# The folded gate and value weights of the last two batch pairs: two engines write their halves where the batches read them, in place of a staging tile and four transfers

## The chip, the cores and the metric

The kernel runs on one core of a Trainium2 chip. The metric is the device time of one execution in microseconds. The core has TensorE (PE in the profile, with its weight loads as PEld), VectorE (DVE), ScalarE (ACT), GpSimd (POOL) and SyncE (SP), and 16 DMA engines that move data between the chip's main memory (DRAM here) and the on-chip buffer. TensorE writes its products into PSUM, from which ScalarE and VectorE read them.

## The reference

Three stages follow each other. The first is an attention with a small packed set of 32 rows per head; the second a gated layer with an RMS norm; the third a two-layer block.

```python
p_packed = sm_attn(p, k, v)                    # q, k, v: (8, 8, 576, 64), p: (8, 8, 32, 64)
x = sm_attn(q, p_packed, p_packed)             # then laid out as (4608, 512)
xn = x / sqrt(mean(x * x) + 1e-6) * rms_g
g, val = xn @ w_gate, xn @ w_val               # 512 -> 1536 each
x = (g * sigmoid(g) * val) @ w_out             # 1536 -> 512
h = x @ w_in                                   # 512 -> 2048
out = maximum(0.01 * h, h) @ w_out2            # 2048 -> 512
```

## The kernel before

**Exact products from two parts.** All large products are made from a high part and a low part of each operand: the helper `mm3` (line 106) issues high x high, low x high and high x low into one PSUM tile, so each product costs three matmuls (their line in the profile is L112). A split is one ScalarE copy to the rounded format (`act_copy`, line 128, L129 in the profile) and one subtraction (`sub`, line 136, L137) on VectorE or GpSimd.

**Folded weights.** The attention's output is the product of the attention rows with `p_packed`, and the kernel does not form it. It multiplies `p_packed` into `w_gate` and `w_val` first. For each pair of batches it keeps a factor tile `lpw` (high and low), and for each block `n` of 256 gate columns and 256 value columns it makes four pieces, `pw_piece` (line 832): one piece is a product of 128 x 128 factors with a 128 x 512 weight tile `w`, three matmuls into a PSUM tile `pwps`. Partitions 0 to 63 of a piece belong to one batch of the pair and partitions 64 to 127 to the other. What is read later is `pw[n, bb]`, one tile for each batch `bb`, with two buffers each.

**How a piece got there.** ScalarE writes the high part of `pwps` over the weight tile `w`, VectorE writes the low part beside it, and two DMAs issued by GpSimd (L858) copy each half's 64 partitions from `w` to the tile of its batch, 256 KB each. So `w` is busy until these DMAs have landed, and there are four buffers of `w`, into which SP loads the next pieces' weights (L763, 512 KB each, four pieces ahead).

**The stages around it.** There are four pairs of batches and six blocks `n` in each, so 24 blocks and 96 pieces. A block is worked off in four steps (two batches, two column halves). In each step `gv` (line 864) makes the gate product `g` and the value product `v` from `pw` and the attention rows `ath`/`atl`, 24 matmuls; ScalarE makes the sigmoid product of `g`, VectorE multiplies it with `v` into `sg`, ScalarE and GpSimd split that into `hh` and `hl`; `y_out` (line 887) then makes 24 matmuls `y<-hh,wo` and `y<-hl,wo` of the step before, and VectorE or ScalarE adds them to `y_acc` (L903, or L129 in a pair's first block). The pieces of block n+1 are made during block n: one after the first step, one after the second, two after the third, none after the fourth. `pwps` and `y` share four PSUM buffers.

The third pair begins after the stretch in which the first half of the last block's layer is worked off (names `zh`, `zo`, `zr`, `zgf`, `zgh`, `zgl`, `zob`), together with the attention of the last four batches; the first four pieces of the third pair and the splits of `ath` for its batches lie in the last steps of that stretch. In the profiled execution the third and fourth pair take from 953.5 to 1301 us. Then the other half of the last layer follows (names `h`, `o`).

**What sets the order.** The code names an order of steps, but the tile framework's scheduler lists the instructions of each engine from it by its own estimates; an engine then works through its list strictly in order, waiting at each instruction for what that needs. So an instruction that waits holds up all that stands behind it on its engine, SP's transfers included.

The weight tile is released and the destination is fixed by these lines:

```python
act_copy(st[:, 0, :], ps)                      # st is w: high part
sub(nc.vector, st[:, 1, :], ps, st[:, 0, :])   # low part
nc.gpsimd.dma_start(out=pw[n, bb][hs, u].bitcast(F32), in_=st[hs].bitcast(F32))
```

Of the kernel before, what the change touches and what calls it, by code (L numbers as in the profile page):

```python
# [26 lines left out]
LATER = (0, 22)  # L27
ZEND = 51
FAST = 8
FASTQ = 6  # L30
OWN = 1
HOLD = 2
# [7 lines left out]
def pack_attention_moe_kernel(  # L40
# [14 lines left out]
    nc = tc.nc  # L55
# [50 lines left out]
    def mm3(ps, terms, start=True, stop=True):  # L106
        seq = [t for hi, lo in (("h", "h"), ("l", "h"), ("h", "l")) for t in [(hi, lo)]]
        n = len(terms) * 3
        i = 0
        for a, b in seq:  # L110
            for (lh, ll), (rh, rl) in terms:
                mm = nc.tensor.matmul(  # L112
                    ps,
                    lhsT=lh if a == "h" else ll,
                    rhs=rh if b == "h" else rl,
                    start=start and i == 0,
                    stop=stop and i == n - 1,
                )
                i += 1
        return mm  # L120
# [7 lines left out]
    def act_copy(o, i, scale=1.0):  # L128
        nc.scalar.activation(out=o, in_=i, func=AF.Copy, scale=scale)  # L129
# [6 lines left out]
    def sub(eng, o, a, hi):  # L136
        eng.tensor_tensor(out=o, in0=a, in1=hi.bitcast(F32), op=ALU.subtract)  # L137
# [67 lines left out]
    def bank(name):  # L205
        return psA.tile([P, 1, 512], F32, tag="y", bufs=ybufs, name=name)
# [18 lines left out]
    def soft1(i):  # L225
# [4 lines left out]
        def keys():  # L230
# [5 lines left out]
            )  # L236
            if i >= FAST:
                st["kh"] = att.tile([P, NS, 2, T], F32R, tag="raw", bufs=raws, name="kh" + nm)
# [9 lines left out]
        def packs():  # L248
# [6 lines left out]
            nc.vector.transpose(out=st["pT"], in_=pm.rearrange("p h (j d) -> p j h d", j=2))  # L255
            if i >= FAST:
                st["ph"] = att.tile([P, 2 * P], F32R, tag="pm", bufs=1, name="ph" + nm)
# [3 lines left out]
        def scores():  # L261
# [4 lines left out]
            for n, (s1, cs) in enumerate(parts):  # L266
                for k_, c in enumerate(cs):
                    if i >= FAST:
                        ss = slice(c * CS, (c + 1) * CS)
# [84 lines left out]
        def packed_turn():  # L354
            PT = att.tile([P, 2, 4, NPK], F32, tag="PT", bufs=2, name="PT" + nm)
            nc.vector.transpose(out=PT, in_=st["Pm"].rearrange("p h (j d) -> p j h d", j=2))
            raw["P", b, u] = (st["Pm"], PT)
            if i >= FAST:
                Ph = att.tile([P, 2 * P], F32R, tag="Ph", bufs=2, name="Ph" + nm)
# [32 lines left out]
    def soft2(i):  # L392
# [14 lines left out]
        def queries(cs):  # L407
# [6 lines left out]
            if cs[-1] == 1:  # L414
                raw.pop(("q", b, u))
                if i >= FAST:
                    st["qh"] = att.tile([P, NS, 2, T], F32R, tag="raw", bufs=raws, name="qh" + nm)
# [5 lines left out]
        def scores(cs):  # L423
            Pm, PT = raw["P", b, u]
            sn = tile_of("sn", "sn", [P, NS, NPK])
            for s2, cs in banks("s2" + nm, b):
                for k_, c in enumerate(cs):
                    if i >= FAST:
                        ss = slice(c * CS, (c + 1) * CS)
# [56 lines left out]
        def turn(cs):  # L486
# [4 lines left out]
            )  # L491
            if i >= FASTQ:
                Pm = raw["P", b, u][0].rearrange("p h d -> p (h d)")
# [10 lines left out]
        def squares(cs, x):  # L504
# [18 lines left out]
            for xp, cs in banks(f"xp{x}" + nm, b):  # L523
                for k_, c in enumerate(cs):
                    if i >= FASTQ:
                        ds, ts = slice(x * P, x * P + P), slice(c * CH, c * CH + CH)
# [125 lines left out]
    def flush_store():  # L652
        if stores:
            o, t = stores.pop()
            nc.sync.dma_start(out=o, in_=t.bitcast(F32))
# [67 lines left out]
    def until(done):  # L723
        while not done():
            assert drip
            drain(1)
# [103 lines left out]
    pw = {}  # L830

    def pw_piece(i):
        if i >= NPAIR * NFG * KT:
            return
        until(lambda: ("s", i) in wq)
        n, kt = i // KT, i % KT
        pr = n // NFG
        u, x = kt // 2, kt % 2
        if kt == 0:
            for bb in range(2):  # L840
                pw[n, bb] = mlpa.tile(
                    [P, 2, 2, 2 * G * P], F32R, tag=f"pw{bb}", bufs=2, name=f"pw{n}{bb}"
                )
        w = wq.pop(("s", i))
        wh, wl = w[:, 0, :], w[:, 1, :]
        lh, ll = lpw[pr]
        ps = bank(f"pwps{i}")[:, 0, :]
        mm3(ps, [((lh[:, kt, :], ll[:, kt, :]), (wh, wl))])

        if stores and stores[0][1] is w:  # L850
            flush_store()
        st = w
        act_copy(st[:, 0, :], ps)
        sub(nc.vector, st[:, 1, :], ps, st[:, 0, :])
        for half in range(2):
            bb = half if x == 0 else 1 - half
            hs = slice(64 * half, 64 * half + 64)
            nc.gpsimd.dma_start(out=pw[n, bb][hs, u].bitcast(F32), in_=st[hs].bitcast(F32))  # L858
# [73 lines left out]
    for f_ in weights[:HOLD]:  # L932
# [6 lines left out]
        (split_wo, 0),  # L939
        (split_wo, 1),  # L940
        (pw_piece, 0),
        (pw_piece, 1),
        (split_w, 4),
        (pw_piece, 2),
        (split_w, 5),
        (pw_piece, 3),
# [170 lines left out]
    for si, (n, bb, c) in enumerate(steps):  # L1117
        pr, fg = n // NFG, n % NFG
# [269 lines left out]
```

## Time and profile before

| what | us |
|---|---|
| median of 3 runs | 1758.36 |
| lowest and highest of them | 1751.75, 1763.99 |
| the profiled execution | 1764.21 |
| its span, first to last instruction | 1762.3 |
| PE busy in it | 1668.8 (95%) |
| DVE, ACT, POOL busy | 915.4, 649.5, 474.4 |

Busy time is the time in which an engine executes instructions, the span's share in brackets. An engine that is busy for 95% over the whole can still stand idle in a stage; a row of the timeline gives behind an instruction, in square brackets, how long its engine had been idle before it and which instruction or transfer ended that.

### The profile page before, as it was taken

How to read it: one execution, taken by the hardware profiler on the slowest of the kernel's cores; microseconds unless marked ns; L12 is line 12 of the kernel's file. 1: busy time of each engine (PE TensorE's matmuls, PEld its weight loads, DVE VectorE, ACT ScalarE, POOL GpSimd, SP SyncE). 2: the span in 40 equal slices, each digit the busy share in tenths (PEclk: the TensorE clock that was granted, in tenths of full speed). 3: DMA queues.
4: the chain of work that ended last, by engine and by line, in shares of the span. 5: the costliest groups of instructions: out<-in, count | busy, mean ns of one | idle time of the engine just before them, and what ended most of it. 6: DMA issues, size and time to landing. Idle time of an engine off the chain costs nothing.

```text
span 1762.3 us, 24309 instructions
## 1 busy us (share of the span) xinstructions
PE 1668.8 (95%) x9252; PEld 1474.4 (84%) x9252; DVE 915.4 (52%) x1560; ACT 649.5 (37%) x1142; POOL 474.4 (27%) x462
## 2 busy tenths in 40 slices
PE   6788889998999999999999899989999999999997
PEld 5578789998998788888888899989998888888885
DVE  6866887776547787666643244324533323232221
ACT  3454654453325555444333322332322222222221
POOL 2454565654421232121223233433310000000000
PEclk9889999999999999999999999999999999999999
DMA  9874776799947463642318657776645101010000
GB/s 280 243 228 145 228 218 192 239 331 324 336 131 271 161 207 127 220 162 76 99 63 281 192 172 204 247 222 186 188 152 212 38 11 38 11 37 13 13 11 24
DMA packets 95527, 287.85 MB, mean 163 GB/s; under 512 B 13876, under 2 KB 20276, under 8 KB 91316
## 3 DMA queue, kind: packets, MB, share of 16 engines
q1 hardware_dynamic: 80052, 235.96, 40.1%
q0 software_dynamic: 15360, 50.34, 11.5%
q8 instruction: 73, 1.20, 0.3%
q14 instruction: 42, 0.34, 0.1%
HBM read 174.85 MB, written 61.08 MB: 134 GB/s over the span
## 4 chain that ended last, share of the span: by engine, by line
PE 75%; DMA 11%; DVE 7%; issue 3%; ACT 2%; POOL 1%; SPq 1%; DVEq 0%; ACTq 0%; POOLq 0%
PE h L112 13%; PE o L112 13%; PE y L112 11%; PE zh L112 8%; PE zo L112 8%; PE g L112 7%; PE v L112 6%; DMA pw<-w 3%; PE pp L335 2%; PE pwps L112 2%; DMA w_dram<-w 1%; PE s L112 1%; DMA v<-in_v_dram 1%; DMA w<-in_moe_w_val_dram 1%; DVE cvw L685 1%
## 5 line engine op out<-in xcount | busy, mean ns | idle before, releaser
L112 PE MATMUL y<-hh,wo 128*128 128x288 f32 x1536 | 271.9, 299 | 9.5 <-DVE w L137 5.0
L112 PEld LDWEIGHTS y<-hh,wo 128*128 128x128 f32 x1536 | 228.6, 190 | 15.9 <-DVE w L137 6.4
L112 PE MATMUL o<-w,gh 128*128 128x512 f32 x640 | 212.4, 392 | 0.0
L137 POOL TENSOR_TENSOR hl<-sg,hh 128x576 fp32r<-128x576 f32 x96 | 139.1, 1449 | 258.0 <-ACT hh L129 252.0
L903 DVE TENSOR_TENSOR y_acc<-y_acc,y 128x288 f32<-128x288 f32 x320 | 140.8, 449 | 124.6 <-PE y L112 123.8
L1300 DVE TENSOR_TENSOR gf<-r,h 128x512 f32<-128x512 f32 x80 | 54.9, 687 | 247.9 <-ACT r L129 247.9
L112 PE MATMUL zo<-w,zgh 128*128 128x512 f32 x512 | 173.0, 394 | 0.0
L112 PE MATMUL g<-ath,pw 128*128 128x288 f32 x768 | 145.6, 305 | 21.4 <-DMA pw<-w 17.8
L112 PE MATMUL h<-yh,w 128*128 128x512 f32 x640 | 162.5, 393 | 0.5 <-DVE y_acc L903 0.5
L112 PE MATMUL zh<-zyh,w 128*128 128x512 f32 x512 | 161.3, 393 | 1.6 <-DVE y_acc L903 1.6
L112 PE MATMUL y<-hl,wo 128*128 128x288 f32 x768 | 162.2, 297 | 0.0
L129 ACT ACTIVATE r<-h 128x512 f32<-128x512 f32 x80 | 47.8, 598 | 260.3 <-PE h L112 260.3
L112 PEld LDWEIGHTS h<-yh,w 128*128 128x128 f32 x640 | 120.0, 188 | 28.2 <-DVE y_acc L903 0.8
L112 PEld LDWEIGHTS g<-ath,pw 128*128 128x128 f32 x768 | 120.0, 194 | 28.0 <-issue 19.6
L112 PE MATMUL v<-ath,pw 128*128 128x288 f32 x768 | 141.1, 298 | 2.0 <-DVE sg L880 2.0
L112 PEld LDWEIGHTS o<-w,gh 128*128 128x128 f32 x640 | 120.1, 188 | 27.1
L858 POOL DMA_DIRECT2D pw<-w x192 | 101.8, 534 | 133.2 <-DVE w L137 102.9
L880 DVE TENSOR_TENSOR sg<-sg,v 128x576 f32<-128x576 f32 x96 | 72.0, 750 | 111.1 <-PE v L112 99.3
L112 PE MATMUL o<-w,gl 128*128 128x512 f32 x320 | 125.0, 391 | 0.0
L112 PEld LDWEIGHTS y<-hl,wo 128*128 128x128 f32 x768 | 124.0, 191 | 0.3
L129 ACT ACTIVATE hh<-sg 128x576 fp32r<-128x576 f32 x96 | 65.7, 684 | 147.8 <-DVE sg L880 140.8
L112 PEld LDWEIGHTS v<-ath,pw 128*128 128x128 f32 x768 | 116.1, 190 | 3.3 <-DVE sg L880 2.6
(159 smaller groups left out, 3064.7 us busy)
## 6 DMA issues: line engine op xcount, KB each, us to landing
pw<-w POOLq DMA_DIRECT2D x192, 256.0 KB, 5.5
w<-w_dram SPq DMA_DIRECT2D x72, 512.0 KB
w<-w_dram SPq DMA_DIRECT2D x32, 1024.0 KB
wo<-wo_dram SPq DMA_DIRECT2D x36, 512.0 KB
w_dram<-w2s SPq DMA_DIRECT2D x32, 512.0 KB
w_dram<-w SPq DMA_DIRECT2D x24, 512.0 KB
y_dram<-y_acc SPq DMA_DIRECT2D x32, 288.0 KB
w<-in_moe_w_in_dram SPq DMA_DIRECT2D x16, 512.0 KB
```

Source lines behind the costliest of these rows:

```text
L112: mm = nc.tensor.matmul(ps, lhsT=lh if a == "h" else ll, rhs=rh if b == "h" else rl, start=start and i == 0, stop=stop and i == n - 1,)
L129: nc.scalar.activation(out=o, in_=i, func=AF.Copy, scale=scale)
L137: eng.tensor_tensor(out=o, in0=a, in1=hi.bitcast(F32), op=ALU.subtract)
L335: nc.tensor.matmul(pp[:, 0, :256], lhsT=st["a1T"][:, j // 3, j % 3, :], rhs=vr[:, :, j, :], start=j == 0, stop=j == NJ - 1,)
L685: nc.vector.scalar_tensor_tensor(out=cu, in0=hiw, scalar=0xC0000000, in1=cu, op0=ALU.bitwise_and, op1=ALU.bitwise_or)
L858: nc.gpsimd.dma_start(out=pw[n, bb][hs, u].bitcast(F32), in_=st[hs].bitcast(F32))
L880: nc.vector.tensor_tensor(out=hf, in0=sg, in1=vps[:, :, :CH], op=ALU.mult)
L903: pace[:] = [nc.vector.tensor_tensor(out=ya, in0=ya, in1=pv, op=ALU.add).ins]
L1300: pace[:] = [nc.vector.tensor_tensor(out=gf, in0=r, in1=ps, op=ALU.max).ins]
```

## The change

A constant `HALVES = 2` is added, and pieces of the third and fourth pair (`pr >= 2`, blocks 12 to 23, 48 of the 96 pieces) take another way. For each half of 64 partitions ScalarE writes the high part from PSUM straight into the batch's `pw` tile, and VectorE subtracts and writes the low part there. The tile `w` is only read by the matmuls, and GpSimd issues no DMA for these pieces. The pieces of the first two pairs stay as they were. Lines behind the first part of the kernel carry a number that is higher by 1, and those behind `pw_piece` one that is higher by 10.

```diff
+HALVES = 2
...
         mm3(ps, [((lh[:, kt, :], ll[:, kt, :]), (wh, wl))])
+        if pr >= HALVES:
+
+            for half in range(2):
+                bb = half if x == 0 else 1 - half
+                hs = slice(64 * half, 64 * half + 64)
+                hi, lo = pw[n, bb][hs, u, 0, :], pw[n, bb][hs, u, 1, :]
+                act_copy(hi, ps[hs])
+                sub(nc.vector, lo, ps[hs], hi)
+            return
```

The lists of all five engines are the same as before up to the first piece of the third pair (about 929 us in the profiled execution), and differ from there to the end of the fourth pair. Three places follow.

ScalarE's list at the end of the stretch before the third pair; `ath_9413` is the split of a batch's attention rows that a transfer brings, `zr_9293` and `zgh_9297` belong to the last step of that stretch, `pwps_8965` and `pwps_9010` are the third and fourth piece. Before:

```order
L129 ACTIVATE w_8884<-pwps_8965 128x512
L129 ACTIVATE zr_9260<-zh_9247 128x512
L129 ACTIVATE zgh_9264<-zgf_9262 128x512
L129 ACTIVATE w_8930<-pwps_9010 128x512
L129 ACTIVATE ath_9413<-atr_8833 128x2x288 x2
L129 ACTIVATE zr_9293<-zh_9280 128x512
L129 ACTIVATE zgh_9297<-zgf_9295 128x512
```

And now:

```order
L130 ACTIVATE zr_9260<-zh_9247 128x512
L130 ACTIVATE zgh_9264<-zgf_9262 128x512
L130 ACTIVATE ath_9413<-atr_8833 128x2x288 x2
L130 ACTIVATE pw_8874<-pwps_8965 64x512
L130 ACTIVATE pw_8875<-pwps_8965 64x512
L130 ACTIVATE pw_8875<-pwps_9010 64x512
L130 ACTIVATE zr_9293<-zh_9280 128x512
L130 ACTIVATE pw_8874<-pwps_9010 64x512
L130 ACTIVATE zgh_9297<-zgf_9295 128x512
```

Both pieces' copies stood ahead of `ath_9413`; now three of their four halves stand between it and `zr_9293`, and the fourth between `zr_9293` and `zgh_9297`.

SP's list in the first steps of the third pair; `w_9470` and `w_9547` are the weights of the eighth and ninth piece of the pair, `zob` the output rows of the stretch before, `wo` the output weights. Before:

```order
L988 DMA w_11335<-w_dram 128x2048
L632 DMA atr_9419<-at_dram 128x1152
L763 DMA w_9470<-w_dram 128x1024
L1009 DMA out_dram<-zob_9125 4x32x512
L1009 DMA out_dram<-zob_9131 2x32x512 x2
L1009 DMA out_dram<-zob_9137 4x32x512
L1009 DMA out_dram<-zob_9143 4x32x512
L795 DMA wo_9472<-wo_dram 128x1024
L763 DMA w_9547<-w_dram 128x1024
```

And now:

```order
L764 DMA w_9470<-w_dram 128x1024
L633 DMA atr_9419<-at_dram 128x1152
L796 DMA wo_9305<-wo_dram 128x1024
L796 DMA wo_9307<-wo_dram 128x1024
L796 DMA wo_9411<-wo_dram 128x1024
L796 DMA wo_9472<-wo_dram 128x1024
L998 DMA w_11335<-w_dram 128x2048
L1019 DMA out_dram<-zob_9125 4x32x512
L1019 DMA out_dram<-zob_9131 2x32x512 x2
L1019 DMA out_dram<-zob_9137 4x32x512
L1019 DMA out_dram<-zob_9143 4x32x512
L764 DMA w_9547<-w_dram 128x1024
```

The loads of `w_9470`, `atr_9419` and `wo_9472` have moved ahead of the stores; `w_9547` stands behind the stores in both.

TensorE's list where the fourth pair begins; `g_11490` is the first product of the pair, `pw_11232` its folded weights, `y_11481` and `y_11497` products of earlier steps. Before:

```order
L112 MATMUL y_11481<-hl_11392,wo_10925 128x288
L112 MATMUL y_11481<-hl_11392,wo_11002 128x288
L112 MATMUL g_11490<-ath_11090,pw_11232 128x288
L112 MATMUL y_11497<-hh_11391,wo_10925 128x288
L112 MATMUL y_11497<-hh_11391,wo_11002 128x288
```

And now:

```order
L113 MATMUL y_11481<-hl_11392,wo_10925 128x288
L113 MATMUL y_11481<-hl_11392,wo_11002 128x288
L113 MATMUL g_11490<-ath_11090,pw_11232 128x288 x4
L113 MATMUL g_11490<-atl_11091,pw_11232 128x288 x2
L113 MATMUL y_11497<-hh_11391,wo_10925 128x288
```

Before, one matmul of `g_11490` stood here, the other eleven behind all `y` matmuls that were ready and a piece; now half of its matmuls stand together here, ahead of `y_11497`.

## Rows read from the trace of the kernel before

**Rows 1.** Stretches from 979.5 us on: length, busy time by engine, granted clock, DMA share.

```profile
core 0: us, PE busy (x) PEld busy (x) DVE busy (x) ACT busy (x) POOL busy (x), PEclk, DMA share, GB/s
...
979.50:986.50 7.00, 0.16 (x2) 0.03 (x1) 0.00 (x0) 0.08 (x1) 0.00 (x0) 0.76 0.57 153
986.50:990.00 3.50, 3.50 (x12) 3.21 (x13) 0.69 (x1) 1.00 (x2) 0.22 (x1) 0.51 0.65 228
990.00:1118.00 128.00, 128.00 (x931) 125.74 (x930) 55.44 (x104) 36.64 (x60) 47.00 (x56) 1.00 0.65 189
...
1161.00:1167.40 6.40, 0.00 (x0) 0.00 (x0) 0.00 (x0) 0.41 (x1) 0.84 (x2) 0.74 0.90 210
1167.40:1170.50 3.10, 3.04 (x13) 3.08 (x14) 0.00 (x0) 0.00 (x0) 0.00 (x0) 0.50 0.65 207
1170.50:1301.20 130.70, 130.70 (x952) 128.52 (x952) 58.92 (x110) 36.59 (x59) 43.16 (x49) 1.00 0.57 164
```

**Rows 2.** Waits of the whole span: us in total, times, longest us.

```profile
PE g L112 <- DMA pw<-w: 17.8, 8, 6.5
...
PE pp L335 <- DMA v<-in_v_dram: 8.0, 2, 4.2
PE pwps L112 <- DMA w<-w_dram: 7.7, 2, 6.8
...
PE y L112 <- DVE w L137: 5.0, 5, 3.1
```

**Rows 3.** Waits between 900 and 1310 us: PE's for a copy.

```profile
PE g L112 <- DMA pw<-w: 7.2, 2, 6.5
```

**Rows 4.** Timeline around the ninth piece of the third pair.

```profile
953.87 14.57 SPq L1009 DMA_DIRECT2D out_dram<-zob  x5
...
971.10 1.04 SPq L763 DMA_DIRECT2D w<-w_dram  x2
...
986.50 0.77 PE L112 MATMUL pwps<-w,lpwh 128*128 128x512 f32 x1 [6.84 <-DMA w<-w_dram]
```

**Rows 5.** Timeline around the first product of the fourth pair.

```profile
1130.66 0.63 PE L112 MATMUL g<-ath,pw 128*128 128x288 f32 x3 [0.75 <-DMA pw<-w]
...
1148.49 0.39 PE L112 MATMUL pwps<-w,lpwh 128*128 128x512 f32 x1
...
1149.04 1.29 DVE L137 TENSOR_TENSOR w<-pwps,w 128x512 fp32r<-128x512 f32 x2 [1.49 <-ACT w L129]
...
1150.03 2.07 POOL L858 DMA_DIRECT2D pw<-w  x4
...
1167.46 1.06 PE L112 MATMUL g<-ath,pw 128*128 128x288 f32 x3 [6.48 <-DMA pw<-w]
```

**Rows 6.** Groups by shape, 990 to 1118 us: busy us, mean ns | idle before; the last of the whole span.

```profile
L903 DVE TENSOR_TENSOR y_acc<-y_acc,y 128x288 f32<-128x288 f32 x68 | 30.5, 453 | 39.2 <-PE y L112 39.2
L137 DVE TENSOR_TENSOR w<-pwps,w 128x512 fp32r<-128x512 f32 x17 | 11.8, 692 | 14.4 <-ACT w L129 14.4
L129 ACT ACTIVATE w<-pwps 128x512 fp32r<-128x512 f32 x17 | 10.2, 598 | 12.9 <-PE pwps L112 12.5
L129 ACT ACTIVATE y_acc<-y 128x288 f32<-128x288 f32 x4 | 1.6, 412 | 2.8 <-PE y L112 2.8
L129 ACT ACTIVATE a1T<-ta 96x384 f32<-96x384 f32 x30 | 13.4, 483 | 4.7 <-PE ta L323 4.7
```

**Rows 7.** Timeline at the end of the stretch before the third pair.

```profile
946.11 0.58 ACT L129 ACTIVATE zr<-zh 128x512 f32<-128x512 f32 x1
...
947.45 0.63 ACT L129 ACTIVATE zgh<-zgf 128x512 fp32r<-128x512 f32 x1 [0.75 <-DVE zgf L1050]
...
948.77 1.29 PE L112 MATMUL zo<-w,zgh 128*128 128x512 f32 x5
950.22 0.50 PE L112 MATMUL zo<-w,zgl 128*128 128x512 f32 x1 [0.16 <-DVE zgl L137]
```

**Rows 8.** The chain that ended last, merged: start us, us, engine and group.

```profile
1301.15 6.40 PE y L112 x48
```

## The prediction

> **What bounds the kernel now.** I read the stretches first, then the waits, then the timeline at the two places that they point to. TensorE is the engine to watch: through the third and fourth pair it is busy without a gap, 128.00 of 128.00 us in one stretch and 130.70 of 130.70 in another, at full clock, while VectorE has 55.44 and ScalarE 36.64 us of work in the first of them [rows 1]. There nothing that the other engines do faster is worth anything, and what they do more costs nothing while it stays in their idle time. The two holes in this stage are what can be won. In one, 979.5 to 986.5 us, TensorE does next to nothing, and in the other, 1161.0 to 1167.4 us, nothing at all [rows 1].
>
> The timeline names what ended each. The first (call it A) is the ninth piece of the third pair, which waited 6.84 us for its weight tile; that load had been issued at 971.10, when SP was through with five stores whose issue had held it from 953.87 on [rows 4]. The second (B) is the first gate product of the fourth pair, which waited 6.48 us for the copies of its folded weights, issued from 1150.03 on; the matmuls of the last piece before had begun at 1148.49 and its low part was done at 1150.3 [rows 5]. A shorter wait of the same kind, 0.75 us, stands at 1130.66 [rows 5]; the two make up all that TensorE waits for copies here, 7.2 us [rows 3]. Behind both holes the granted clock is at the lower of its two levels, 1.2 GHz: 0.51 over 3.5 us and 0.50 over 3.1 us [rows 1].
>
> **The change part by part.** *The copies go.* 96 DMAs of 256 KB and their waits leave the third and fourth pair. For B this is the whole cause: the same data is to be written by ScalarE and VectorE. The last two pieces' matmuls begin their last one at 1148.49, and 0.39 us later four high parts and four low parts are due. At one instruction of 0.60 us after the other on ScalarE, and the last subtraction of 0.69 us behind, they are ready at about 1148.9 + 4 x 0.60 + 0.69 = 1152.0. TensorE's new list has 48 matmuls between that piece and the first product, which take 6.40 us [rows 8], so it comes there at about 1155.3. That is 3.3 us to spare. Gain: 6.48 us, the lost half of 3.1 us at half clock (1.55), and the 0.75 us at 1130.66 by the same argument.
>
> *The weight tile is free earlier.* It is released by the piece's matmuls and no longer by the landing of the copies, so SP, whose list stands still at a load without a free tile, comes through earlier, and the DMA engines have no copies to move beside it. The load of hole A took 986.5 - 971.1 = 15.4 us [rows 4]. It still stands behind the five stores, but the transfers that filled the queue in front of them are issued earlier. On the other side, counted in the lists, TensorE has 24 matmuls more in front of that piece (198 now from the third pair's first product on, 174 before); at 6.40 us for 48 that is 3.2 us, so it now comes there at 979.66 + 3.2 = 982.9 instead of 979.66. Best case: the load lands before, gain 6.84 us. Worst case: it is issued and lands as before, and 986.5 - 982.9 = 3.6 us of waiting stay, gain 3.2 us. I take the best, because either an issue 4 us earlier or a landing 4 us faster is enough. With the hole goes half of 3.5 us at half clock (1.7); all of it in the best case, nothing in the worst.
>
> The Trainium skill, in "DMA: Bandwidth & Descriptors", section "Issuing engines are not separate DMA queues", says that DMAs of all issuing engines run on the same 16 DMA engines and interleave. By that rule copies that are gone let the load through, and A's 8.5 us are won. The trace agrees only in part: the engines' mean share in the hole itself was 0.57, not full [rows 1], which is why the worst case above stays among the rivals.
>
> *Two instructions in place of one, on ScalarE and on VectorE.* Each is 64 partitions by 512 columns. The trace has no instruction on 64 partitions of that length. Lower bound: half the time, so nothing is added. Upper: the same time as on 128 partitions, 0.598 and 0.692 us [rows 6]. I take the upper, since ScalarE's 96 x 384 took 483 ns, which lies on the line through 128 x 288 (412) and 128 x 512 (598) at 492 [rows 6]: the columns set the time. So ScalarE gets 48 x 0.598 = 28.7 us and VectorE 48 x 0.692 = 33.2 us more over some 350 us. In the stretch from 990 us, with 17 pieces, VectorE goes from 55.4 to 67.2 and ScalarE from 36.6 to 46.8 of 128 us: TensorE stays the bound, and its work is what covers both. What uncovers them is the third rival.
>
> *The end of the stretch before.* Three halves now stand on ScalarE between the split of the attention rows and the copy `zr` of the last step, and a fourth between `zr` and `zgh`. So `zr` moves from 946.11 to at most 946.11 + 3 x 0.60 = 947.9. It takes 0.58, the fourth half 0.60 and `zgh` 0.63, so `zgh` ends at 949.7 instead of 948.1, and the matmuls that need it, the last four of the five that began at 948.77, were due at 949.0 [rows 7]: 0.7 us late, with the handovers between engines 0.9. Bounds: the split in front of them comes 1.8 us earlier because its rows are loaded without copies beside them, and even the 0.16 us of waiting at 950.22 go; or two more subtractions of 0.69 stand in front on VectorE, 2.3 us. I take a loss of 0.9.
>
> GpSimd loses 96 DMA issues, and nothing waits for GpSimd at either hole; I set that at nothing.
>
> **The sum.** B: 6.48 + 1.55 + 0.75 = 8.8. A: 6.84 + 1.7 = 8.5. End of the stretch before: -0.9. Together 16.4 us, so 1764.21 - 16.4 = 1747.8 for an execution like the profiled one. That execution is 5.85 us above the median of the runs, 1758.36. If the excess lies in waits for transfers, the part of these in the two holes is (6.84 + 7.2) of the 33.5 us that TensorE waits for transfers in the three largest groups (17.8 + 8.0 + 7.7) [rows 2], 42% or 2.5 us, and the median run has that much less to win: 1758.36 - 13.9 = 1744.5. I say 1744, 0.8% less than before. About 1% is what a measurement of this kernel can tell from no change, so the forecast lies just inside.
>
> **The rivals.**
>
> *B goes, A stays in part.* The load is slow by itself or is issued as late as before. For it: the DMA engines were not full in the hole, and the load stands behind the same stores. Against it: the earlier release, 3.2 us more of work in front, no copies. Of A only 3.2 us are won: 1758.36 - (8.8 + 3.2 - 0.9 - 2.5) = 1750.
>
> *The freed transfers give more.* The runs differ by 12 us among themselves, and what differs could be waits for transfers of this stage rather than of the start; a median run would then win what the profiled one wins, and the end of the stretch before wins its 0.16 us: 1758.36 - 17.5 = 1741, or a little below.
>
> *The first product of each block waits for the engines (slower).* The last two pieces of a block are made 48 matmuls, 6.40 us, before the next block's first product. If the four high and four low parts don't overlap (4 x (0.598 + 0.692) = 5.2 us) and a `y_acc` addition is taken in between each (4 x 0.453 = 1.8), with two other ScalarE instructions of 0.6 us in front, the data comes after 8.2 us, 1.8 us late, at each of the 11 block changes: 20 us. From 1.5 us at each (16.4 / 11) the change is slower. 20 - 16.4 = 3.6 us over the time before, about 1762. For it: TensorE did wait for this subtraction to give a PSUM buffer back, 5 times and 5.0 us in the whole span [rows 2]. Against it: none of those waits lies in this stage, and both engines are idle for more than half of it.
>
> **How the numbers follow.** The forecast 0.60, B alone 0.18, more gain 0.14, slower 0.08. The range holds the first two rivals and is cut inside the last: 1735 to 1758. Faster by over 1% means below 1740.8: most of the second rival (0.12) and two fifths of the forecast (0.24), whose gain is uncertain by some 5 us; together 0.36. Slower by over 1% needs a price of 34 us and more in the third rival, well over what I worked out: 0.04. Within 1%: 0.60.
>
> **What would show it.** Right: no wait of a gate product for a copy behind 929 us; TensorE busy without a gap and at full clock from the third pair's second step to the end of the fourth pair; the two new instructions at 0.60 and 0.69 us each; VectorE at about 52% between the holes. Wrong: a wait of the ninth piece for its load of 3 us or more; waits of `g` for VectorE's subtraction at the block changes; waits of `y` for it; a `zgh` that comes more than 2 us later than TensorE. If both holes are gone and the time is still that of before, the gain was lost ahead of 929 us, where nothing is changed, or in the last stage.

## The result, and the profile after

The changed kernel takes 1740.91 us (median of 6 runs, 1737.57 to 1745.53), the kernel before 1758.32 (median of 6, 1751.75 to 1763.99). The ratio is 0.9906, 95% interval 0.9881 to 0.9932; the medians lie 17.4 us apart. The forecast was 1744, range 1735 to 1758. The profiled execution after took 1740.60 us, its span is 1738.8 us, 23.5 us less than the span before.

Three marks split both spans: the first matmul of the third pair's first piece, the first gate product of that pair, and the first product `h` of the last stage.

| part | before | after | difference |
|---|---|---|---|
| start to first piece | 929.76 | 925.04 | -4.72 |
| first piece to first gate product | 23.76 | 23.31 | -0.45 |
| third and fourth pair | 354.56 | 336.27 | -18.29 |
| last stage | 454.22 | 454.18 | -0.04 |

The change is in the second and third row. In the first row the lists are the same in both kernels; it differs from execution to execution. In the two pairs both holes are gone. The stretches of the profile after, in the columns of [rows 1]:

```profile
953.50:990.00 36.50, 36.50 (x267) 35.83 (x266) 12.84 (x20) 19.30 (x39) 8.59 (x6) 1.00 0.39 142
990.00:1118.00 128.00, 128.00 (x930) 125.63 (x929) 71.17 (x128) 47.02 (x76) 31.32 (x22) 1.00 0.34 121
1118.00:1180.00 62.00, 62.00 (x451) 60.81 (x450) 27.43 (x46) 27.78 (x52) 12.86 (x9) 1.00 0.48 181
```

TensorE (first figure) is busy through all of each, at a granted clock of 1.00, where before it stood still for 7 and 6.4 us and then ran at half clock [rows 1]. VectorE has 71.17 us of work in the middle stretch, 56%, where 52% was forecast. All that TensorE waits for between 900 and 1310 us (total, times, longest), beside [rows 3]:

```profile
PE g L113 <- DVE zob L1086: 1.2, 1, 1.2
PE h L113 <- DVE y_acc L913: 0.5, 1, 0.5
PE pwps L113 <- DMA w<-w_dram: 0.4, 1, 0.4
```

Hole A is looked at where [rows 4] were. The timeline of SP and of the ninth piece after:

```profile
946.53 9.10 SPq L1019 DMA_DIRECT2D out_dram<-zob  x5
...
955.73 23.00 SPq L764 DMA_DIRECT2D w<-w_dram  x5
...
977.52 0.40 PE L113 MATMUL pwps<-w,lpwh 128*128 128x512 f32 x1
```

The five stores hold SP for 9.10 us, not 14.57, and the ninth piece's load is issued at 955.73, which is 7.4 us behind the pair's first gate product (948.35). Before it was 17.6 us (971.10 against 953.52). TensorE comes to the piece 29.2 us behind that product and waits for nothing.

The issue comes 10.2 us earlier by three things. The first store is issued 2.2 us earlier against that product (before, SP waited until 953.37 for the copies that held the eighth piece's tile). The stores hold SP 5.5 us less; that was no wait for their data, as the last `zob` addition had ended at 953.47. And a `wo` load of 2.44 us, which stood between them and the piece's load, has moved ahead of the stores in SP's new list. The ninth piece's own tile is none of the three: before, the copies that held it had landed at 967.05, 4 us ahead of the issue.

The trace also records when each of a load's 16 parts lands. Before, twelve had landed at 975.98, and the last four followed from 979.98 to 986.37, 15.3 us behind the issue. After, twelve had landed at 961.00 and the last four followed from 961.89 to 967.66, 11.9 us behind the issue and 9.9 us ahead of TensorE.

Hole B, where [rows 5] were. The prediction calls it the fourth pair's first product; by the trace it stands one block later. The trace has 1152 gate matmuls, 48 for each block. Counted by them the pair's first product begins at 1125.88 (the 0.75 us wait at 1130.66 is in it) and that of its second block at 1155.09, with the rest of its matmuls at 1167.46. ScalarE's `y_acc` copies, which only a pair's first block has, agree:

```profile
1125.88 0.29 PE L112 MATMUL g<-ath,pw 128*128 128x288 f32 x1
...
1140.47 0.41 ACT L129 ACTIVATE y_acc<-y 128x288 f32<-128x288 f32 x1 [2.34 <-PE y L112]
```

What ended the hole stays as it was read: the last of the copies issued from 1150.03 on took 15.7 us to land, where the median of all copies is 5.5. The same place after:

```profile
1133.51 1.11 ACT L130 ACTIVATE pw<-pwps 64x512 fp32r<-64x512 f32 x2
...
1133.59 0.40 PE L113 MATMUL pwps<-w,lpwh 128*128 128x512 f32 x1
...
1134.12 2.04 DVE L138 TENSOR_TENSOR pw<-pwps,pw 64x512 fp32r<-64x512 f32 x3 [1.47 <-ACT pw L130]
...
1136.68 0.69 DVE L138 TENSOR_TENSOR pw<-pwps,pw 64x512 fp32r<-64x512 f32 x1 [0.52 <-ACT pw L130]
...
1140.20 0.69 PE L113 MATMUL g<-ath,pw 128*128 128x288 f32 x4
```

The last low part is ready at 1136.68 + 0.69 = 1137.37, and the second block's first gate product begins at 1140.20: 2.8 us to spare.

The groups by shape, 990 to 1118 us (busy us, mean ns, idle before), answer to [rows 6]:

```profile
L913 DVE TENSOR_TENSOR y_acc<-y_acc,y 128x288 f32<-128x288 f32 x73 | 33.2, 455 | 34.8 <-PE y L113 34.5
...
L138 DVE TENSOR_TENSOR pw<-pwps,pw 64x512 fp32r<-64x512 f32 x36 | 24.8, 689 | 11.6 <-ACT pw L130 11.0
...
L130 ACT ACTIVATE pw<-pwps 64x512 fp32r<-64x512 f32 x36 | 21.3, 593 | 7.3 <-DVE pw L138 6.0
```

Half the partitions cost what all 128 cost. Last, the end of the stretch before the third pair, beside [rows 7]:

```profile
937.60 1.26 ACT L130 ACTIVATE ath<-atr 128x576 fp32r<-128x576 f32 x2 [1.38 <-DMA atr<-at_dram]
...
941.21 0.58 ACT L130 ACTIVATE zr<-zh 128x512 f32<-128x512 f32 x1
...
942.78 0.63 ACT L130 ACTIVATE zgh<-zgf 128x512 fp32r<-128x512 f32 x1
```

Counted from the first piece, `zr` stands at 16.2 us (941.21 - 925.04), before at 16.4: it did not move.

### The profile page after: what moved, and what is told of

Read it like the earlier page. It is cut to its first block, busy times and chain, and to the rows that moved or that the text cites. A ratio compares the mean times of both kernels' runs of the same rounds, so it can differ in the third digit from the quotient of the medians.

```text
span 1738.8 us, 24013 instructions
## 1 busy us (share of the span) xinstructions
PE 1662.0 (96%) x9252; PEld 1468.5 (84%) x9252; DVE 948.7 (55%) x1608; ACT 676.8 (39%) x1190; POOL 424.4 (24%) x366
## 4 chain that ended last, share of the span: by engine, by line
PE 74%; DMA 12%; DVE 7%; issue 2%; ACT 2%; SPq 1%; POOL 1%; DVEq 0%; ACTq 0%; POOLq 0%
PE h L113 13%; PE o L113 13%; PE y L113 12%; PE zo L113 8%; PE zh L113 7%; PE g L113 7%; PE v L113 7%; DMA pw<-w 3%; PE pwps L113 3%; PE pp L336 2%; DMA w_dram<-w 2%; DMA w<-in_moe_w_val_dram 2%; DMA w<-in_moe_w_in_dram 1%; PE s L113 1%; DVE cvw L686 1%
## 5 line engine op out<-in xcount | busy, mean ns | idle before, releaser
L113 PEld LDWEIGHTS y<-hh,wo 128*128 128x128 f32 x1536 | 226.2, 189 | 15.8 <-DVE w L138 5.5
L113 PE MATMUL g<-ath,pw 128*128 128x288 f32 x768 | 141.2, 302 | 12.8 <-DMA pw<-w 9.7
L113 PEld LDWEIGHTS zh<-zyh,w 128*128 128x128 f32 x512 | 95.1, 188 | 21.3 <-DVE y_acc L913 2.1
```

Source lines behind the costliest of these rows:

```text
L113: mm = nc.tensor.matmul(ps, lhsT=lh if a == "h" else ll, rhs=rh if b == "h" else rl, start=start and i == 0, stop=stop and i == n - 1,)
```

## Experiments

The theory to test: two holes, each with a cause in its own pair (B: the products waited for copies; A: a load came late because copies held the weight tile and filled the queues), and engine work that TensorE covers. Of each run one execution was profiled. Below, "the two pairs" is the time from the first gate product of the third pair to the first `h`, read from the timelines: 354.56 before, 336.27 after.

**One pair at a time.** `fourth_only` is the first edit, `third_only` the second:

```diff
-HALVES = 2
+HALVES = 3
```

```diff
-        if pr >= HALVES:
+        if pr == HALVES:
```

> Only the fourth pair's pieces (blocks 18 to 23) are split directly; the third pair's are copied as before. Theory (each hole has its cause in its own pair): the hole before the ninth piece of the third pair stays, 5 to 9 us with the half clock behind it, and the hole at the first product of the fourth pair goes, 8.8 us. Third and fourth pair together about 354.6 - 8.8 = 345.8 us, time about 1758 - 9 = 1749. Rival (the first hole is closed by the newly scheduled lists, whatever way the third pair's pieces take): both holes gone, pair stretch about 337 us, time about 1741. Rival (TensorE would have lost the time somewhere else): no change, 1758.

> Only the third pair's pieces (blocks 12 to 17) are split directly; the fourth pair's are copied as before. Theory: the first hole goes (8.5 us), the wait of the fourth pair's first product for its copies stays, about 6.5 us and 1.5 us of clock; pair stretch about 354.6 - 8.5 = 346 us, time about 1749 to 1750. Rival (copies wait only because there are so many of them in the queues): the second hole shrinks to 2 us or less, and the time is about 1743.

Measured: `fourth_only` 1750.96 us, ratio 0.9966 (0.9945 to 0.9986), the two pairs 347.83 us. `third_only` 1750.06 us, ratio 0.9976 (0.9950 to 1.0003), the two pairs 345.51 us. The timeline of `fourth_only` (SP, then TensorE) at the ninth piece:

```profile
950.79 13.93 SPq L1019 DMA_DIRECT2D out_dram<-zob  x5
964.77 2.44 SPq L796 DMA_DIRECT2D wo<-wo_dram  x1
967.38 17.28 SPq L764 DMA_DIRECT2D w<-w_dram  x4
...
983.79 0.76 PE L113 MATMUL pwps<-w,lpwh 128*128 128x512 f32 x1 [7.34 <-DMA w<-w_dram]
```

Hole A is back almost as it was (7.34 for 6.84 us), although the fourth pair's lists are the new ones. In `third_only` it is gone, and B stands at the fourth pair's second block, with a price that had not been expected behind it:

```profile
1149.88 1.06 PE L113 MATMUL g<-ath,pw 128*128 128x288 f32 x3 [3.01 <-DMA pw<-w]
...
1228.79 0.69 DVE L138 TENSOR_TENSOR yl<-yl,yh 128x512 fp32r<-128x512 f32 x1 [6.04 <-ACT yh L1108]
...
1229.90 0.79 PE L113 MATMUL y<-hh,wo 128*128 128x288 f32 x4 [3.43 <-DVE y_acc L913]
```

B is 3.0 us here, not 6.5. Later VectorE stands for 6 us at a split whose input a transfer brings late, the `y_acc` addition behind it on its list comes late, and TensorE waits 3.4 us for that. The single gains of the two pairs are 6.7 and 9.0 us, together 15.8 of the 18.3. The two blocks around each hole, from the first gate product of one block to that of the second block behind it, show why it is not all:

| run | A: third pair's first two blocks | B: fourth pair's first two blocks |
|---|---|---|
| before | 953.52 to 1013.15, 59.63 | 1125.88 to 1191.52, 65.64 |
| after | 948.35 to 999.35, 51.00 | 1112.03 to 1168.37, 56.34 |
| `fourth_only` | 949.53 to 1011.64, 62.11 | 1124.76 to 1181.11, 56.35 |
| `third_only` | 948.52 to 999.48, 50.96 | 1112.15 to 1173.88, 61.73 |

Where its own pair is split directly, a hole's blocks take what they take in the changed kernel: A is worth 8.6 us and B 9.3, together 17.9 of the 18.3. What differs is the hole that stays, 2.5 us longer for A and 3.9 shorter for B, and the later wait. By medians the two runs gain 4.9 and 5.8 us of 17.4, less than the stretches say, and the interval of `third_only` reaches 1: its runs spread over 13 us (1746.62 to 1760.03). So the traces show that each hole belongs to its pair; the medians alone would not.

**The copies brought back without a reader.** Three kernels keep the direct split and add transfers by GpSimd for each of the 48 pieces; `spill` is scratch space in DRAM that nothing reads:

```diff
+            spill = dram.tile([P, 2, 512], F32, name=f"spill{i}")
+            for half in range(2):
+                hs = slice(64 * half, 64 * half + 64)
+                nc.gpsimd.dma_start(out=spill[hs], in_=w[hs].bitcast(F32))
```

That is `copies_held`. In `copies_free` the source is `w_dram[i % NW][hs]`; in `held_small` it is `w[hs, 0]` with `hs` of only 4 partitions.

> The direct split as in the changed kernel, and beside it GpSimd copies both halves of the weight tile of each of the 48 pieces to a scratch place in DRAM that nobody reads, 256 KB each: the transfers and the later release of the weight tile are back, and no product waits for them. Theory (the first hole came of the transfers and of the tile that they held): a wait of a piece for its weights, 3 to 8 us around the ninth piece of the third pair, comes back, with a lower clock behind it; no hole at the fourth pair's first product; time about 1741 + 5 to 8 = 1746 to 1750. Rival (the first hole was due only to the place that the scheduler had given to things): no hole, 1741.

> As the run with copies from the weight tile, but the source of the 96 transfers of 256 KB is the same weights in DRAM: the traffic is back, the weight tile is released by the matmuls. SP's list is that of the changed kernel. If the holding of the tile makes the first hole: no hole, about 1741. If the traffic makes it: a wait of 3 us or more for a weight load in the third pair, 1746 to 1750 or above, since each transfer both reads and writes DRAM.

> The direct split, and beside it two transfers of 8 KB from the weight tile of each piece to DRAM: the tile is held for as long as such a transfer takes to land, nearly without traffic. If holding as such makes the first hole: SP comes to the ninth piece's load later by some us, a wait of up to 3 us, 1742 to 1745; if the traffic is needed for it: no wait, 1741.

Measured: `copies_held` 1746.44 us, ratio 0.9935 (0.9920 to 0.9950), the two pairs 343.64; `held_small` 1748.87, ratio 0.9953 (0.9938 to 0.9968), the two pairs 344.21; `copies_free` 1781.12, ratio 1.0127 (1.0095 to 1.0159), the two pairs 336.24. The first has the time that the theory gave it, and for another reason. GpSimd and TensorE in its timeline:

```profile
969.04 1.11 POOL L861 DMA_DIRECT2D spill<-w  x2 [12.84 <-DMA w<-w_dram]
...
971.42 1.41 POOL L138 TENSOR_TENSOR hl<-sg,hh 128x576 fp32r<-128x576 f32 x1
...
972.88 0.85 PE L113 MATMUL y<-hl,wo 128*128 128x288 f32 x2 [4.31 <-POOL hl L138]
```

No piece waits for its weights there, though the copies and the later release are back. GpSimd, in order on its list, stands 12.84 us at a transfer whose tile has not been loaded, the split `hl` stands behind it, and TensorE waits for `hl`. In `held_small` the same:

```profile
957.71 17.44 SPq L764 DMA_DIRECT2D w<-w_dram  x3
...
970.17 1.02 POOL L861 DMA_DIRECT2D spill<-w  x2 [10.86 <-DMA w<-w_dram]
...
972.66 0.85 PE L113 MATMUL y<-hl,wo 128*128 128x288 f32 x2 [5.27 <-POOL hl L138]
```

So both are misses for hole A. The load took 11.9 us in both (issued at 956.67 and landed at 968.52 in `copies_held`, 957.71 and 969.65 in `held_small`), as in the changed kernel. That says nothing of copies beside it, because there were none: while it was under way GpSimd stood at its transfer. The DMA queues from 956.7 to 968.5 us in `copies_held`, and from 971.1 to 986.4 us in the kernel before, where the load took 15.3 us (packets, MB, share of the 16 engines; q1 is SP's queue, q0 GpSimd's):

```profile
q1 hardware_dynamic: 894, 2.67, 66.9%
q8 instruction: 1, 0.02, 0.8%
...
q1 hardware_dynamic: 724, 2.26, 45.8%
q0 software_dynamic: 321, 1.05, 32.5%
```

What does come back in `copies_held` is a longer issue of the stores: 12.58 us, where it was 14.57 before, 13.93 in `fourth_only` and 9.10 after. (In `held_small` it is 6.91; why less than after was not found.) Even so the load, issued 10.9 us behind the pair's first product, is there in time. SP's list is the new one there, with the `wo` loads and the eighth piece's load ahead of the stores, so the order that the scheduler gave SP may be part of what closed A. The old order without copies was not run, and the two are not separated.

`copies_free` tells nothing of hole A. Its transfers need no tile, and GpSimd had issued all 96 before 333 us, beside the work of the first pairs, which lost the time: the third pair's first piece stands at 967.01 us instead of 925.04.

**What the load stands behind.** A stretch of the profile after in which SP's stores are nearly all that moves (last three figures: granted clock, share of the 16 DMA engines, GB/s):

```profile
954.20:958.20 4.00, 4.00 (x30) 3.86 (x29) 1.82 (x3) 2.08 (x4) 1.84 (x2) 1.00 0.26 101
```

The stores keep a quarter of the DMA engines busy, for a long time, and four parts of the load behind them come late. The Trainium skill, "DMA: Bandwidth & Descriptors", section "Why a DMA increments its semaphore by 16 and not by 1", says that a DMA is spread over the largest number of engines up to 16 that divides the outer dimension of both sides. The stores' outer dimension is 4 or 2, so by that rule at most 4 of the 16 are busy; the trace agrees with 0.26 and with four late parts. A load that has a part on every engine then has those on the stores' few engines queued behind them. That would explain 12 to 16 us for a load. The next run is `fourth_only`, with the five stores issued by GpSimd.

```diff
-            nc.sync.dma_start(
+            eng.dma_start(
...
-                store_rows(i * 4 + t, obz[t], slice(0, DM))
+                store_rows(
+                    i * 4 + t, obz[t], slice(0, DM), nc.gpsimd if i == NZ - 1 else nc.sync
+                )
```

> As the run with the fourth pair alone split directly, but the five stores of output rows that stand in SP's list ahead of the ninth piece's load are issued by GpSimd; the rest of SP's list is unchanged. Theory (the first hole came of the load's late issue, 17 to 18 us behind the pair's first product, because SP was busy issuing the stores for 14 us): the load is issued within 4 us of the pair's first product, the wait of 7.3 us goes, with the clock behind it: third and fourth pair 337 to 341 us instead of 347.8, time about 8 us below the 1751 of that run, 1743. Rival (the load is late because the copies' transfers lie in front of it, whenever it is issued): the wait stays at 4 us or more and the time above 1747. GpSimd's copies of the sixth piece now stand behind the stores on its list, so a wait of a gate product for copies of 1 to 3 us may come instead.

Measured: 1742.64 us, ratio 0.9925 (0.9900 to 0.9949), the two pairs 338.0. GpSimd, SP and TensorE in its timeline (first gate product at 951.40):

```profile
949.85 3.51 POOL L1019 DMA_DIRECT2D out_dram<-zob  x5 [2.37 <-DVE zob L1086]
...
969.47 8.96 SPq L764 DMA_DIRECT2D w<-w_dram  x3
...
977.41 0.40 PE L113 MATMUL pwps<-w,lpwh 128*128 128x512 f32 x1
```

The time and the closed hole are as the theory had them, the mechanism is not. The load is issued as late as in `fourth_only`, 18.1 us behind the first product (17.9 there): SP waited 16.3 us for the copies to give the tile back. But it lands 3.7 us later (at 973.19), where it took 16.3 in `fourth_only`, and copies were under way beside it. The view of `zob` and the DMA queues from 969.5 to 973.2 us:

```profile
DMA to landing us min/median/max: 11.8/15.0/15.8
...
q1 hardware_dynamic: 145, 0.53, 41.5%
q0 software_dynamic: 83, 0.29, 33.7%
```

The last store was issued at 952.66, so all five had landed ahead of the load's issue. A load that met no stores took 3.7 us with copies beside it; one behind stores took 11.9 without copies and 15.3 and 16.3 with them (before, `fourth_only`). So the stores in front are the larger part. The 3.4 to 4.4 us more with both may be the copies or the `wo` load that there stands right ahead of it; the runs do not separate them.

So hole A needed two things: a late issue and a slow way. In `fourth_only`, as before, SP's stores and the `wo` load set the issue (the tile was back at 963.83, 3.6 us ahead of it); here the tile does. The change issues the load 10.2 us earlier and shortens its way by 3.3 us; this run takes 12.6 us from its way alone. Since the load met no stores at all here, the run does not tell whether another queue helps while stores are still under way. Stores laid out over all 16 engines were not tried.

**The engine work.** `twice` makes each half's copy and subtraction two times:

```diff
-                act_copy(hi, ps[hs])
-                sub(nc.vector, lo, ps[hs], hi)
+                for _ in range(2):
+                    act_copy(hi, ps[hs])
+                    sub(nc.vector, lo, ps[hs], hi)
```

> Each half's copy and subtraction is made twice with the same result, so the two engines get another 28.7 and 33.2 us over the third and fourth pair. Theory (TensorE covers both engines, with 2.8 us to spare at a block change): VectorE rises from 56% to about 65% in the third pair; the last parts come 4 x 0.69 = 2.8 us later at a block change, so waits of the first product of 0 to 1 us at each of 11 changes, time 1741 to 1752. Rival (the first product of each block is already at the edge, waiting being hidden by its order): 2.5 us and more at each of 11 changes, 28 us, 1769. If the engines have room to overlap, no change at all, 1741.

Measured: 1753.79 us, ratio 0.9982 (0.9965 to 0.9998), the two pairs 347.16, more than the 1752 that the theory allowed. The work added is 96 instructions on each engine, 66 and 57 us, twice what the expectation wrote. VectorE has 91.93 us in the stretch of 128, 72%, and TensorE's waits in the two pairs are:

```profile
PE y L113 <- DVE y_acc L914: 2.4, 3, 1.3
PE y L113 <- DVE pw L138: 1.2, 7, 0.2
```

No wait of `g` at a block change, so the slower rival of the prediction finds no support even at twice the work. What comes instead are waits of `y`, whose PSUM buffers VectorE frees late. They make 3.6 of the 10.9 us lost in the two pairs; 2.7 us more is the half clock at the third pair's start (granted 0.50; the first 24 matmuls of `g` and `v` take 6.1 us instead of 3.4), behind a wait of 3.5 us for `zob`. The other 4.6 us are in no wait that the trace lists.

`highs_first` writes both high parts of a piece before both low parts. In the changed kernel the program puts a semaphore between the first low part and the second high part, and ScalarE waited there 20 times.

```diff
                 act_copy(hi, ps[hs])
-                sub(nc.vector, lo, ps[hs], hi)
+                parts.append((lo, ps[hs], hi))
+            for lo, p, hi in parts:
+                sub(nc.vector, lo, p, hi)
```

> The two high parts of a piece are written first, then the two low parts (in the changed kernel the second high part waits for the first low part, by a semaphore in the program: 20 waits, 13.5 us of ScalarE's time in the two pairs). Theory: those waits go, and as TensorE has 2.8 us to spare at the block change it is worth nothing: 1741 within 2 us. Rival (the engines' parts are on the path): up to 0.7 us at each of 11 block changes, 1733.

Measured: 1743.25 us, ratio 0.9916 (0.9902 to 0.9931), the two pairs 336.28, as in the changed kernel. ScalarE's and VectorE's waits on each other in the two pairs, after:

```profile
DVE pw L138 <- ACT pw L130: 35.9, 37, 1.5
ACT pw L130 <- DVE pw L138: 13.5, 20, 0.8
```

and in `highs_first`, where the second kind no longer occurs:

```profile
DVE pw L138 <- ACT pw L130: 50.0, 33, 2.7
```

The 13.5 us have gone over to VectorE's side, and no idle time of these two engines is on the path here.

**More pairs.** `second_too` sets `HALVES = 1`, `all_pairs` sets `HALVES = 0`. The first was timed once alone and then, as `second_again`, beside the changed kernel (`after_again`) and `all_pairs` on one chip.

> The second pair's pieces are split directly too (72 of 96 pieces). Theory: the waits of the gate product for copies in the second pair, 0.5 + 4.5 = 5.0 us in the run after the change, go, and no new waits come as VectorE is busy for 58 to 69 of 100 us there and gets 17 us more over some 190 us: the time is 4 to 7 us below the changed kernel's 1741, about 1735. Rival (VectorE and ScalarE are busy enough there, with attention work, that the halves come late): the same waits with another name, for VectorE's or ScalarE's part, and a time of 1741 or more.

> The changed kernel once more, beside the next two on the same chip: 1741, within 3 us.

> The second pair split directly too, once more, to set it against the changed kernel on the same chip. If the waits for copies in the second pair are really won: 3 to 5 us below the changed kernel in the same rounds. If the difference of the first comparison was that of chips: equal within 2 us.

> All 96 pieces are split directly, the first pair's too. There VectorE is busy for 70 to 84 of 100 us already and would get 16.6 us more over some 200 us. Theory (the change is worth something only where the two engines have idle time): the waits for copies in the first pair, 5.2 us in the profile of the changed kernel, go, but attention work comes later by as much or more; no better than the run with the second pair, 1735 to 1745. Rival (TensorE's order leaves room there too): 4 to 5 us below that run, about 1731.

| run | us | ratio to before (95%) |
|---|---|---|
| `second_too` | 1736.62 | 0.9891 (0.9855 to 0.9928) |
| `after_again` | 1742.18 | 0.9923 (0.9899 to 0.9948) |
| `second_again` | 1735.20 | 0.9880 (0.9855 to 0.9905) |
| `all_pairs` | 1730.76 | 0.9854 (0.9828 to 0.9879) |

The second pair gives 7.0 us more, as the theory had it. The first gives another 4.4, against the theory that VectorE had no room there: that run's rival was right, with runs that overlap a little (1732.01 to 1738.48 and 1727.48 to 1733.48). Two stretches of the first two pairs in `after_again`:

```profile
100.00:300.00 200.00, 175.72 (x1106) 161.41 (x1105) 154.38 (x270) 100.06 (x182) 110.17 (x98) 0.97 0.67 204
300.00:500.00 200.00, 189.20 (x1343) 183.34 (x1342) 127.79 (x221) 82.62 (x142) 101.08 (x104) 0.99 0.89 282
```

and in `all_pairs`:

```profile
100.00:300.00 200.00, 180.99 (x1114) 163.76 (x1114) 172.42 (x294) 119.72 (x209) 92.20 (x64) 0.96 0.49 165
300.00:500.00 200.00, 195.27 (x1412) 190.74 (x1410) 148.56 (x250) 97.84 (x169) 79.02 (x55) 1.00 0.60 216
```

VectorE goes from 154 to 172 of 200 us and TensorE still does 5.3 and 6.1 us more work. TensorE's largest wait from 60 to 600 us in `after_again`, against its largest in `all_pairs`:

```profile
PE g L113 <- DMA pw<-w: 8.6, 4, 4.1
```

```profile
PE s L283 <- DVE pw L138: 5.3, 2, 3.4
```

The copies' waits go, and other waits for VectorE stand there instead. `all_pairs` beats both kernels: 25.9 us below the one before in the same rounds.

## Why the prediction was right

**B, 8.8 us: right.** The forecast put the last low part 3.3 us ahead of the first product, the trace has 2.8. Its two blocks are 9.3 us shorter, in `fourth_only` as in the changed kernel. The place was named one block too early: the hole is at the first product of the pair's second block, and the 0.75 us wait at the first of all. B by itself varies, though: 3.4 us of waits for copies in `third_only` where before had 7.2.

**A, 8.5 us: right, its reason in part.** Its two blocks are 8.6 us shorter. The best case was taken because either an issue 4 us earlier or a landing 4 us faster would do. The issue is 10.2 us earlier against the pair's first product (7.4 for 17.6 us), and the landing 3.3 us faster (11.9 for 15.3). The piece itself is reached 3.0 us later, forecast 3.2. The release of its own tile did not set the issue before: SP's stores and a `wo` load did, and the release of the tile before it gave part of 2.2 us. What makes the load slow is for the larger part the stores ahead of it, which the prediction saw and counted only in its first rival. That copies that are gone let the load through, by the rule of the Trainium skill that the prediction quotes, accounts for 3.3 us of its way at most.

**The end of the stretch before, -0.9 us: wrong sign.** It came out at +0.45, beyond the lower bound of 0.16. The step put three halves between the split of the attention rows and `zr` and let the split stand where it was. It came 2.6 us earlier, 12.6 us behind the first piece instead of 15.2. SP issued the load of its rows at the same place, 8.7 us behind the first piece (933.77 after, 938.48 before), but from the issue to the split it was 3.8 us instead of 6.5. The loads of rows without copies beside them had been named as the reason for the lower bound, with 1.8 us.

**Two instructions in place of one: right.** Half the partitions take 592 and 688 ns, the upper bound. VectorE has 948.7 us of work over the span for 915.4, 33.3 more (forecast 33.2), ScalarE 27.3 more (28.7).

**The sum, 16.4 for the profiled execution: 18.7 measured** in the two rows of the table that the change touches: 0.45 at the end of the stretch before and 18.3 in the two pairs, of which A's blocks are 8.6, B's 9.3 and the other blocks 0.3.

**The median run, 13.9: 17.4 measured, 14.5 in the second measurement** (`after_again`, 1742.18 for 1756.69). Their intervals are 12 to 21 and 9 to 18 us, so both hold the forecast, and the times do not settle this step. It gave 42% of the profiled execution's excess of 5.85 us to the two holes. The profiles speak for another place. In the ten profiled executions of kernels that leave all ahead of the third pair as it was (without `copies_free`, whose transfers run there), that pair's first piece stands at 921.1 to 929.8 us, median 925.2; in the one of before it is at 929.76. The two pairs themselves, once the copies are out, repeat to 0.03 us (336.25 to 336.28 in six executions of four kernels). If a median run of the kernel before has its first piece at 925.2 too, 4.6 of the 5.85 us come ahead of the change, and it wins nearly what the profiled one does: 18.7 less about 1.3 is 17.4. How the holes vary from run to run in the kernel before is not shown, as it was profiled once.

The second rival's 1741 is the time measured, but not by its reason. It put what differs between runs into this stage rather than the start, and the profiles differ at the start: that it hit the number is luck.

## What to carry to other kernels

A copy that only moves data to where the next step reads it costs by when it lands: look at which product waits for it, which load waits for the buffer that it holds, and what else stands in that load's queue. A store that few engines carry can hold a load behind it for longer than the copies do. How busy an engine is does not tell by itself whether it can take the copies' place: VectorE at 72% cost time where it held up PSUM buffers (`twice`), and at 86% it still gained where copies had been waited for (`all_pairs`). Before a difference of a profiled execution is spread over its waits, split the span at marks and see where repeated executions differ.

## What the runs showed of the hardware

Five stores whose outer dimension is 4 or 2 kept 0.26 of the DMA engines busy at 101 GB/s. Of a 512 KB load issued behind them on the same queue twelve of 16 parts landed within 4.9 to 6.3 us and the last at 11.9 us (eleven executions without copies beside it), 15.3 and 16.3 (two with copies); where the stores had landed all 16 took 3.7 us. ScalarE and VectorE take as long for 64 partitions by 512 as for 128 (592 and 688 ns against 591 and 682, means of the changed kernel). A transfer that GpSimd issues holds all that stands behind it for as long as its source is not there, 10.9 and 12.8 us here, where VectorE's and ScalarE's lists went on.
